# Moving the casts of expert 0's weights by three turns inside attention

## The chip, the cores and the metric

The kernel runs on one core of a Trainium2 chip. The metric is the time of one execution on the device in microseconds; the median of 3 runs of the kernel before is 624.77 us (624.53 to 625.55). Engine names: PE is TensorE (PEld its weight loads), DVE VectorE, ACT ScalarE, POOL GpSimd, SP SyncE.

## The reference

Three layers follow one another on 2 sequences of 768 tokens:

```
scores = q @ k.T / sqrt(64) + bias;  a = softmax(scores, masked)     # 8 heads, the last 96 keys and 8 global ones
x = a @ v                                                            # (2, 768, 512)
e = argmax(x @ w_gate), or the expert of the token before            # 8 experts, one per token
x = p[e] * (relu(x @ w1[e]) @ w2[e])
u = x + real(fft(fft(x, axis=1), axis=2))
out = u + relu(layernorm(u) @ w_ch1) @ w_ch2
```

All in float32. The expert of a token depends on a scan over the sequence.

## The kernel before

Attention works on 24 units, numbered n from 0 to 23: a unit is one tile of 128 queries (i, six of them), one sequence (b) and one half of the heads (g, four heads). The loop at L292 is software-pipelined: in its pass n it issues `scores` (PE, L152) and `rowmin` (DVE, L161) of unit n, the exponentials `expo` (ACT, four at L170, with `den` on POOL at L171 right behind them), the transposes `transp` (PE, L180) of unit n-1 in two halves, each copied out of PSUM by ACT (`out`, L186, tile `p`), the products with v (PE, L194) of unit n-2, and the turning back of unit n-3 (`keep` on DVE, L199, tile `o`; `upright` on PE, L204; `norm` on DVE). Every engine runs its instructions in the order in which the program issues them, so the place of a call in this loop is its place in the queue of its engine.

Four times in a pass, `step(k)` is called, with k = 4 (n - 24) and the three numbers after it: these are the four turns of a unit, 0 to 3. Turn 0 lies between `scores` and `expo`, turn 1 after the first `out`, turn 2 after the second half of `transp`, turn 3 at the end of the pass. In a turn, `bg.step()` advances every background generator by one step, the oldest first. Two kinds of generators are of interest:

- `route.run(i)` (L486), one per tile of queries, added after the last unit of a tile has been normalised, which is in turn 2 of pass 4i+6. It finds the expert of each token. For tiles 0 to 3 part of it is on POOL: `gn` (L532, read by PE at L551), `pe` (L548, read by ACT at L556), `su` (L562, read by DVE at L569), `oh` (L571), `xrow` (L593) and two indirect DMAs to `list` (L607). It waits for given turns (`to`, `at`).
- `ring.take("e", g, cols=512, eng=POOL)` (L1005), for expert 0's pieces g = 0, 1, 2. A piece is 128 x 2048 floats of weights in a raw buffer, loaded by DMA earlier (SP, L990). It is split into a rounded high part, a cast on ACT (L1052), and a low part, a subtraction on POOL (L1054), in four parts of 512 columns: cast, subtraction, cast, subtraction, one per turn. After the last subtraction the raw buffer's next load is issued. The high and low parts are first read by PE after attention, at L897.

`TAKES` (L672) says at which k each of the three generators is added. With (-53, -37, -21) this is turn 3 of passes 10, 14 and 18, so the casts fall in turns 3, 1, 3, 1 and the subtractions in turns 0, 2, 0, 2.

After attention the routing of the last tile, the scattering of tokens to the experts' lists, the eight experts, the Fourier step and the last layer follow.

Of the kernel before, what the change touches and what calls it, by code (L numbers as in the profile page):

```python
# [80 lines left out]
def fast_attention(tc, st, io, route):  # L81
# [4 lines left out]
    with ExitStack() as ctx:  # L86
# [189 lines left out]
        def step(k):  # L276

            for at, g in TAKES:
                if k == at:
# [389 lines left out]
EARLY_READ = 7  # L669
EARLY_GATHER = 6  # L670
LATE = 4
TAKES = ((-53, 0), (-37, 1), (-21, 2))  # L672
SPLIT = 6
WARM = 6, 6, 3
TOKENS = 4
# [1282 lines left out]
```

## Time and profile before

| | |
|---|---|
| median of 3 runs | 624.77 us |
| the profiled execution's own time | 628.3 us |
| its span, first to last instruction | 626.5 us |
| PE busy in the span | 606.2 us (97%) |
| DVE busy | 382.9 us (61%) |
| ACT busy | 274.1 us (44%) |
| POOL busy | 100.7 us (16%) |

Busy shares are means over stages with different limits: POOL is busy for 13.20 us of the 20 between 40 and 60 us, and nearly idle after 200 us. Times in the rows are counted from the span's start. In a timeline row stand start, length, engine, line, operation, tiles written and read, their shapes, the number of instructions merged into the row, and in brackets how long the engine had been idle before it and what released it. Lengths of instructions that follow one another on an engine overlap a little.

### The profile page before, as it was taken

The page shows a single profiled execution, that of the slowest core. Times are in us where ns is not written, and L with a number is a line of the kernel's source. Part 1 is how long each engine was busy: PE and PEld are TensorE (multiplying, and loading weights), DVE is VectorE, ACT ScalarE, POOL GpSimd, SP SyncE. Part 2 cuts the span into 40 slices and gives each one's busy share as a digit, 9 for nine tenths or more (in the row PEclk, how much of TensorE's full clock was granted, in tenths as well). Part 3 has the DMA queues.
Part 4 walks back from the last instruction along what each step waited for, and adds up shares of the span by engine and source line. Part 5 has one row for each costly group of instructions (what it writes and reads, how often), then busy time and mean ns, then how long its engine had stood idle before and what let it go on. Part 6 is the DMA issues. An engine that isn't in the chain of part 4 may idle for free.

```text
span 626.5 us, 9659 instructions
## 1 busy us (share of the span) xinstructions
PE 606.2 (97%) x3515; PEld 493.5 (79%) x3516; DVE 382.9 (61%) x897; ACT 274.1 (44%) x547; POOL 100.7 (16%) x149
## 2 busy tenths in 40 slices
PE   8999988899999899999999999999999999999997
PEld 4777875598898788887767887888888888888885
DVE  6788775569876958671499979997430221372112
ACT  6889883166564766573344534431211221131010
POOL 2146652324224033300000000000000000000000
PEclk9999999999999899999999999999999999999999
DMA  8568761399979788980450343560100100100001
GB/s 285 194 197 210 205 118 61 56 336 336 385 273 329 248 293 309 322 281 9 184 186 2 135 154 116 201 202 0 68 1 1 68 0 1 67 1 1 0 1 67
DMA packets 25186, 92.44 MB, mean 148 GB/s; under 512 B 7644, under 2 KB 8796, under 8 KB 17184
## 3 DMA queue, kind: packets, MB, share of 16 engines
q1 hardware_dynamic: 19664, 79.50, 38.4%
q0 software_dynamic: 4736, 10.56, 4.6%
q10 hardware_dynamic: 720, 1.55, 0.7%
q8 instruction: 34, 0.56, 0.4%
q14 instruction: 32, 0.26, 0.2%
HBM read 81.00 MB, written 14.84 MB: 153 GB/s over the span
## 4 chain that ended last, share of the span: by engine, by line
PE 51%; DVE 1%; ACT 0%; issue 0%; DVEq 0%; ACTq 0%
PE h L1759 21%; PE acc L1774 7%; PE acc L1775 7%; PE acc L1776 7%; PE y L1211 1%; PE acc L1593 1%; PE acc L1579 1%; PE h L1261 1%; PE f L1725 1%; PE f L1622 1%; PE h L52 1%; PE f L1644 0%; DVE u L1785 0%; PE acc L1582 0%; PE f L1625 0%; PE acc L1644 0%
## 5 line engine op out<-in xcount | busy, mean ns | idle before, releaser
L1764 DVE SCALAR_TENSOR_TENSOR hl<-h,hh 128x512 fp32r<-128x512 f32 x48 | 33.0, 688 | 118.0 <-ACT hh L1763 118.0
L1763 ACT ACTIVATE hh<-h 128x512 fp32r<-128x512 f32 x48 | 28.7, 598 | 164.9 <-PE h L1759 164.9
L1054 DVE TENSOR_TENSOR wide<-raws,wide 128x1024 fp32r<-128x1024 f32 (+1 forms) x38 | 44.7, 1198 | 28.9 <-ACT wide L1052 23.1
L170 ACT ACTIVATE t<-t,nm 128x256 f32<-128x256 f32 (+1 forms) x96 | 45.8, 479 | 10.9 <-DVE nm L161 10.1
L1052 ACT CAST wide<-raws 128x1024 fp32r<-128x1024 f32 (+2 forms) x42 | 40.7, 992 | 8.6 <-DMA raws<-wm 4.3
L1759 PE MATMUL h<-un0h,wide 128*128 128x512 f32 (+1 forms) x136 | 42.4, 378 | 0.1
L1774 PE MATMUL acc<-wide,hh 128*128 128x512 f32 (+1 forms) x97 | 37.9, 391 | 0.0
L1775 PE MATMUL acc<-wide,hh 128*128 128x512 f32 (+1 forms) x97 | 37.9, 390 | 0.0
L1776 PE MATMUL acc<-wide,hl 128*128 128x512 f32 (+1 forms) x97 | 37.6, 388 | 0.0
L161 DVE CUSTOM_DVE_ANT_0 t<-sp,bias 128x256 f32<-128x256 f32 (+1 forms) x96 | 32.8, 397 | 7.7 <-PE sp L152 3.8
L1140 POOL DMA_INDIRECT xg<-xs,ent x23 | 27.5, 1197 | 44.1 <-DVE pc L1187 21.4
L1759 PEld LDWEIGHTS h<-un0h,wide 128*128 128x128 f32 x136 | 25.0, 188 | 5.0 <-ACT un0h L1534 0.3
L180 PE MATMUL tp<-consts,t 128*128 128x128 f32 x176 | 26.2, 284 | 2.8 <-ACT p L186 2.8
L180 PEld LDWEIGHTS tp<-consts,t 128*128 128x128 f32 x176 | 18.6, 141 | 10.6 <-ACT p L186 6.6
L1759 PE MATMUL h<-un0l,wide 128*128 128x512 f32 (+1 forms) x68 | 25.6, 377 | 0.0
L194 PE MATMUL sm<-p,vs 128*64 128x128 f32 x352 | 24.5, 280 | 0.0
L186 ACT COPY p<-tp 128x512 f32<-128x512 f32 (+1 forms) x48 | 24.2, 534 | 0.3 <-PE tp L180 0.3
L1231 PE MATMUL h<-xh,wide 128*128 128x256 f32 x160 | 22.6, 280 | 0.0
L1103 DVE SCALAR_TENSOR_TENSOR dec<-raws,dec 128x1024 int32<-128x1024 int32 x18 | 22.0, 1225 | 0.6
L1101 DVE SCALAR_TENSOR_TENSOR dec<-raws,dec 128x1024 int32<-128x1024 int32 x18 | 22.0, 1223 | 0.5
L194 PEld LDWEIGHTS sm<-p,vs 128*64 128x64 f32 x352 | 18.7, 136 | 3.7 <-issue 3.6
L1234 ACT ACTIVATE hh<-h 128x512 fp32r<-128x512 f32 x20 | 12.0, 599 | 21.6 <-PE h L1231 16.5
(474 smaller groups left out, 1606.6 us busy)
## 6 DMA issues: line engine op xcount, KB each, us to landing
raws<-we SPq DMA_DIRECT2D x32, 1024.0 KB
raws<-wm SPq DMA_DIRECT2D x17, 1024.0 KB
raws<-wmf SPq DMA_DIRECT2D x7, 1024.0 KB
wmf<-dec POOLq DMA_DIRECT2D x8, 512.0 KB
xs<-xrow SPq DMA_DIRECT2D x12, 260.0 KB
vs<-v SPq DMA_DIRECT2D x6, 512.0 KB
raws<-kq SPq DMA_DIRECT2D x3, 1024.0 KB
u<-x SPq DMA_DIRECT2D x6, 512.0 KB
```

What stands on the lines that cost most here:

```text
L161: V.tensor_tensor_reduce(out=u.t[:, x, :u.W], in0=u.sp[:, j, k, :u.W], in1=bias[:, 4 * u.g + x, u.b0:u.b0 + u.W], scale=-0.125, scalar=3.0 ...
L170: A.activation(u.t[:, x, :u.W], u.t[:, x, :u.W], AF.Exp, bias=u.nm[:, x:x + 1], scale=-1.0, accum_out=u.den[:, x])
L180: T.transpose(u.tp[k][:, j, c], u.t[:, 2 * k + j, c * P:(c + 1) * P], st.ident)
L194: T.matmul(turned[j * D:j * D + D, k], vs[:, ti % KS, u.h + 2 * k + j], u.p[:, 2 * k + j, c], start=c == 0, stop=c == len(tiles) - 1)
L1052: (first or nc.scalar.copy)(hi[:, cs], raw[:, cs])
L1054: (eng() if callable(eng) else eng or nc.vector).tensor_tensor(lo[:, cs], raw[:, cs], hi[:, cs].bitcast(F32), op=ALU.subtract)
L1759: nc.tensor.matmul(ps[:, c], a[:, k], x[:, k, c], start=n == 0, stop=n == 11)
L1763: nc.scalar.activation(hh, ps, AF.Relu)
L1764: nc.vector.scalar_tensor_tensor(hl, ps, 0.0, hh.bitcast(F32), op0=ALU.max, op1=ALU.subtract)
L1774: T.matmul(acc[c][:, d], hh[:, cs], h2[:, d], start=first, stop=False)
L1775: T.matmul(acc[c][:, d], hh[:, cs], l2[:, d], start=False, stop=False)
L1776: T.matmul(acc[c][:, d], hl[:, cs], h2[:, d], start=False, stop=last and d.stop == DM)
```

## The change

One line: each of the three generators is added three calls of `step` sooner, in turn 0 of the same pass. The casts then fall in turns 0, 2, 0, 2 (the first and third), the subtractions in turns 1, 3, 1, 3.

```
-TAKES = ((-53, 0), (-37, 1), (-21, 2))
+TAKES = ((-56, 0), (-40, 1), (-24, 2))
```

Since the generator of a piece is now added in turn 0 of pass 10, before `route.run(1)` in turn 2 of the same pass, it also stands before that one in the list that `bg.step()` goes through.

On POOL, around the first piece, the kernel before has this order; the first `den` is that of unit 10, `list` and its two DMAs belong to the routing of tile 0, `gn`, `pe` and `su` to that of tile 1, and `sl0l` is the low part of the piece:

```order
L171 TENSOR_SCALAR den<-den 128x4
L607 DMA list<-dest,pos 12416x2 x2
L532 TENSOR_SCALAR gn<-lg 128x16
L124 COPY raws<-gk 128x4x8
L1054 TENSOR_TENSOR sl0l<-raws,sl0h 128x512
L171 TENSOR_SCALAR den<-den 128x4
L548 TENSOR_TENSOR pe<-lg,m_709 128x16
L1054 TENSOR_TENSOR sl0l<-raws,sl0h 128x512 x2
L171 TENSOR_SCALAR den<-den 128x4
L562 TENSOR_SCALAR su<-su 128x2
```

And the changed kernel, from the same `den` to the same `su`:

```order
L171 TENSOR_SCALAR den<-den 128x4
L1054 TENSOR_TENSOR sl0l<-raws,sl0h 128x512
L607 DMA list<-dest,pos 12416x2 x2
L1054 TENSOR_TENSOR sl0l<-raws,sl0h 128x512
L532 TENSOR_SCALAR gn<-lg 128x16
L124 COPY raws<-gk 128x4x8
L171 TENSOR_SCALAR den<-den 128x4
L1054 TENSOR_TENSOR sl0l<-raws,sl0h 128x512
L548 TENSOR_TENSOR pe<-lg,m_713 128x16
L1054 TENSOR_TENSOR sl0l<-raws,sl0h 128x512
L171 TENSOR_SCALAR den<-den 128x4
L562 TENSOR_SCALAR su<-su 128x2
```

Two subtractions have moved ahead of `gn`, a third ahead of `pe`, and the fourth ahead of `su`'s `den`; before, one stood ahead of `pe`, three ahead of `su`'s `den` and the fourth behind `su`.

On ACT, before, from the exponentials of unit 10 to those of unit 12; `sl0h` is the high part of the piece, `rows` and the small `pe` belong to the routing of tile 1:

```order
L170 ACTIVATE t,den<-t,nm 128x256 x4
L186 COPY p<-tp 128x512
L1052 CAST sl0h<-raws 128x512
L186 COPY p<-tp 128x512
L170 ACTIVATE t,den<-t,nm 128x256 x4
L186 COPY p<-tp 128x512
L1052 CAST sl0h<-raws 128x512 x2
L186 COPY p<-tp 128x512
L555 COPY rows<-sm 16x256
L556 ACTIVATE pe<-pe 128x16
L170 ACTIVATE t,den<-t,nm 128x256 x4
```

And after, from the cast that now stands ahead of the exponentials of unit 10:

```order
L1052 CAST sl0h<-raws 128x512
L170 ACTIVATE t,den<-t,nm 128x256 x4
L186 COPY p<-tp 128x512
L1052 CAST sl0h<-raws 128x512
L186 COPY p<-tp 128x512
L1052 CAST sl0h<-raws 128x512
L170 ACTIVATE t,den<-t,nm 128x256 x4
L186 COPY p<-tp 128x512
L1052 CAST sl0h<-raws 128x512
L186 COPY p<-tp 128x512
L555 COPY rows<-sm 16x256
L556 ACTIVATE pe<-pe 128x16
```

The two casts that stood together between two copies of `p` are apart, two casts stand ahead of exponentials, and the fourth cast, which came after the exponentials of unit 12, comes before them. The order on PE, SP and DVE is the same in both kernels. The second and third piece move in the same way, four units later each.

## Rows read from the trace of the kernel before

**Rows 1.** Windows view, 40 to 60 us; columns: stretch, length, engines' busy times, PEclk, DMA share, GB/s.
```profile
core 0: us, PE busy (x) PEld busy (x) DVE busy (x) ACT busy (x) POOL busy (x), PEclk, DMA share, GB/s
40.00:60.00 20.00, 19.66 (x202) 15.30 (x196) 16.74 (x87) 18.25 (x60) 13.20 (x22) 1.00 0.72 196
```
**Rows 2.** Timeline of PE, first piece.
```profile
45.41 0.22 PE L551 MATMUL sm<-identb,gn 128*16 128x128 bf16 x1
...
46.61 0.66 PE L180 MATMUL tp<-consts,t 128*128 128x128 f32 x4 [0.34 <-ACT p L186]
...
48.73 1.13 PE L152 MATMUL sp<-raws 64*128 64x256 f32 x8
...
52.70 1.13 PE L152 MATMUL sp<-raws 64*128 64x256 f32 x8
```
**Rows 3.** Timeline of ACT, first piece: exponentials of units 10 to 13 and two casts.
```profile
38.63 0.51 ACT L170 ACTIVATE t<-t,nm 128x256 f32<-128x256 f32 x1 [0.80 <-DVE nm L161]
...
42.49 0.51 ACT L170 ACTIVATE t<-t,nm 128x256 f32<-128x256 f32 x1 [0.32 <-DVE nm L161]
...
44.94 1.14 ACT L1052 CAST sl0h<-raws 128x512 fp32r<-128x512 f32 x2
...
46.83 0.49 ACT L170 ACTIVATE t<-t,nm 128x256 f32<-128x256 f32 x1
...
50.71 0.51 ACT L170 ACTIVATE t<-t,nm 128x256 f32<-128x256 f32 x1 [0.35 <-DVE nm L161]
```
**Rows 4.** Timeline of POOL, first piece.
```profile
40.86 0.23 POOL L171 TENSOR_SCALAR den<-den 128x4 f32<-128x4 f32 x1 [2.97 <-ACT t L170]
41.84 1.19 POOL L607 DMA_INDIRECT list<-dest,pos  x1 [0.76 <-DVE gf L539]
43.34 0.98 POOL L607 DMA_INDIRECT list<-dest,pos  x1 [0.30 <-issue]
44.32 0.31 POOL L532 TENSOR_SCALAR gn<-lg 128x16 bf16<-128x16 f32 x1
...
44.71 1.30 POOL L1054 TENSOR_TENSOR sl0l<-raws,sl0h 128x512 fp32r<-128x512 f32 x1
46.10 0.23 POOL L171 TENSOR_SCALAR den<-den 128x4 f32<-128x4 f32 x1
46.41 0.22 POOL L548 TENSOR_TENSOR pe<-lg,m 128x16 f32<-128x16 f32 x1
46.58 2.62 POOL L1054 TENSOR_TENSOR sl0l<-raws,sl0h 128x512 fp32r<-128x512 f32 x2
49.29 0.22 POOL L171 TENSOR_SCALAR den<-den 128x4 f32<-128x4 f32 x1
49.59 0.23 POOL L562 TENSOR_SCALAR su<-su 128x2 f32<-128x2 f32 x1
```
**Rows 5.** Timeline of DVE, first piece: the instruction that waits for su.
```profile
49.85 0.17 DVE L569 RECIPROCAL su<-su 128x2 f32<-128x2 f32 x1 [1.01 <-POOL su L562]
```
**Rows 6.** Timelines of POOL and PE, second and third piece: den, gn and L551.
```profile
56.70 0.23 POOL L171 TENSOR_SCALAR den<-den 128x4 f32<-128x4 f32 x1 [2.75 <-ACT t L170]
...
59.79 0.29 POOL L532 TENSOR_SCALAR gn<-lg 128x16 bf16<-128x16 f32 x1
...
61.27 0.22 PE L551 MATMUL sm<-identb,gn 128*16 128x128 bf16 x1
...
72.85 0.23 POOL L171 TENSOR_SCALAR den<-den 128x4 f32<-128x4 f32 x1 [3.42 <-ACT t L170]
...
75.94 0.28 POOL L532 TENSOR_SCALAR gn<-lg 128x16 bf16<-128x16 f32 x1
...
77.39 0.22 PE L551 MATMUL sm<-identb,gn 128*16 128x128 bf16 x1
```
**Rows 7.** Timeline of DVE, third piece: the copy of o behind L569.
```profile
83.64 0.42 DVE L199 COPY o<-sm 128x256 f32<-128x256 f32 x1 [1.66 <-PE tp L180]
```
**Rows 8.** Windows view of two microseconds after attention: clock and PE.
```profile
108.00:109.00 1.00, 1.00 (x3) 0.81 (x4) 0.61 (x2) 0.00 (x0) 0.71 (x1) 0.50 0.45 168
124.00:125.00 1.00, 0.00 (x0) 0.00 (x0) 1.00 (x1) 0.00 (x0) 0.00 (x0) 1.00 0.72 262
```
**Rows 9.** Windows view, 37.0 to 37.5 us: DMA traffic.
```profile
37.00:37.50 0.50, 0.50 (x6) 0.46 (x8) 0.50 (x2) 0.50 (x2) 0.41 (x2) 1.00 0.23 98
```

## The prediction

> **What bounds the kernel now.** I first read the windows view by stage, since the edit touches only the stretch from 37 to 84 us of the span. There TensorE is busy 19.66 of 20 us, ScalarE 18.25, VectorE 16.74 and GpSimd 13.20 [rows 1]; GpSimd's share of the whole span is small, but in this stretch it is two thirds. Then I read the timeline of one unit around expert 0's first piece, engine by engine. A unit's PE work, from one `scores` to the next, is about 4 us (48.73 to 52.70) [rows 2]. Where PE stops in it, it stops for ScalarE: the second half of the transposes at 46.61 stood 0.34 us for the copy of `p`, and that copy stood behind two casts in a row, 1.14 us from 44.94 [rows 2, 3]. GpSimd's work in these units is not slack either: gn (L532), pe (L548) and su (L562) of the routing lie in its queue, and PE (L551), ScalarE (L556) and VectorE (L569) wait for them. GpSimd runs its queue in order, so what stands ahead of these three counts.
>
> **The change part by part.** Nothing is added or removed. Per piece, four casts (a pair takes 1.14 us) and four subtractions on GpSimd move three turns up; this happens three times. The pieces' next loads stand where they stood in SP's queue and are released earlier.
>
> ScalarE's side is a gain. No two casts stand together between the halves of a `p` copy any more, so the copy at the end of the pair comes one cast sooner, and PE's 0.34 us go. The moved casts now stand ahead of the exponentials. There ScalarE was idle 0.80 us in unit 10 and 0.32 us in unit 11, waiting for nm [rows 3]; a cast takes half the pair, 0.57 us, of which the first is hidden whole and the second costs at most 0.25 us of ScalarE.
>
> GpSimd's side is the cost. Before, unit 10's queue is den, two L607, gn, and only then a subtraction. Now one subtraction stands between den and the first L607, a second between the last L607 and gn, and a third between the next den and pe. I rebuild the queue of the first piece [rows 4]. Den at 40.86; the step from den to the next instruction is 0.31 us (46.10 to 46.41): first subtraction at 41.17. It takes 1.30: end 42.47. L607 after 0.30 of issue (the idle of its second row): 42.77 instead of 41.84, since the 0.76 us that GpSimd idled there hide a part. From the first L607 to gn it was 2.48 us (41.84 to 44.32), so the second subtraction begins at 45.25; with 1.30 and 0.09 to the next instruction (46.01 to 46.10), gn begins at 46.64 and ends at 46.95, 2.32 us later than before.
>
> - PE: L551 stood at 45.41 [rows 2]; it cannot start before 46.95, 1.54 us later, and the transposes, `upright`, `values` and next `scores` queue behind it on PE. The 0.34 us of waiting for `p` are absorbed in this, so `scores` at 48.73 comes 1.20 us later. This is the lower end.
> - ScalarE: gn to the next group was 0.39 us (44.32 to 44.71), so den follows at 47.03, the third subtraction at 47.34, pe at 48.73 to 48.95 [rows 4]. The exp of pe (L556) stands in ScalarE's queue right ahead of the exponentials of unit 12; these begin 0.1 us after it, about 49.1 instead of 46.83 [rows 3]: 2.27 us later. This is the upper end.
> - VectorE: den before came at 49.29, 2.46 us after those exponentials began, 0.39 of it because a subtraction ended only at 49.20. Now the last subtraction (48.9 to 50.2) is over in time: den 51.2, su 51.5, and L569, which came 0.26 us after su began, 51.8 instead of 49.85 [rows 4, 5]. Behind L569 stand the copy of `o`, for which PE's `upright` waits, and the next `rowmin`, for which the exponentials of unit 13 (50.71) wait [rows 3]. PE has some 0.5 us between that copy and its `upright`, so unit 14's `scores` (52.70) [rows 2] comes about 1.5 us later. Unit 13 has no cast left and no second subtraction, and PE works through it without a wait, so little is won back there.
>
> I take 1.5 us per piece, between 1.2 and 2.3. The second and third piece stand the same way: gn came 3.09 us after den both times, 3.46 in the first; by the same steps gn moves from 59.79 to about 62.4 and from 75.94 to about 78.6, past L551 at 61.27 and 77.39 [rows 6]. For the third piece I take 1.0 only: behind its L569 VectorE stands 1.66 us more, until 83.64, for a reason that the trace does not give (the named PE instructions were begun and the copy usually follows at once) [rows 7]. If that wait ends at a fixed moment, the delay disappears in it; if it has a fixed length, it stays. Sum: 1.5 + 1.5 + 1.0 = 4.0 us. After attention everything hangs on its last unit (routing, list, gathers), so I pass the 4.0 us on whole.
>
> The profiled execution took 628.3 us (span 626.5 and 1.8 around it), 3.5 above the median of the runs, 624.77. 632.3 over 628.3 is 1.0064; on the median that is 628.8 us. Bounds of the mechanism: 2.4 us (two pieces at the lower end, the third lost in that wait) to 6.9 (three at the upper end): 627.2 to 631.7.
>
> **The rivals.**
>
> 1. Faster. The pair of casts is the only thing that PE waits for, and GpSimd's lateness reaches nobody. Then each piece wins PE's 0.34 us of waiting and up to the 0.57 us of one cast, about 0.43 us: 1.3 us in all, 623.5 us. For it: the wait for `p` is PE's only visible one in unit 12, and GpSimd idles long ahead of den. Against it: den stays ahead of the first subtraction, so that idle time cannot be used, and gn would have to be done at 45.41, that is, lose 0.78 us at most; I count 2.32. It decides from there.
> 2. No change: the ScalarE gain and a GpSimd delay of under one subtraction cancel, 624 to 625.5 us. This needs gn's delay to be about 1.2 us, half of what I find; subtractions beside other engines' work would have to be shorter than their rows.
> 3. A slower clock. TensorE has a hole of 1.5 us per piece. At 108 us its granted clock is 0.50, the 1.2 GHz level, after several microseconds in which it was often idle; but from 124 to 125 us it was idle for the whole microsecond and stayed at 1.00 [rows 8]. I expect no fall. If it fell in each piece for the about 3.5 us of the stretch at 108, PE would lose half of that, 1.75 us, three times: 634 us.
> 4. The first cast now wants its data at 37.8 us. The load of that piece runs together with others; traffic has fallen to 98 GB/s at 37.0 to 37.5 [rows 9], so I take it as landed. Should it land 1 us late, the first cast would hold back exponentials that start at 38.63 by 0.7 us, once: 629.5 us, inside the forecast's range.
>
> On rival 3, the Trainium skill ("TensorE: Matmul & The Clock Gate", Part 1: The HAM clock gate) says that a gate halves the matmul clock after the array has been idle and gives it back after sustained work. By that rule a change that opens holes in TensorE's work pays twice, as worked out in rival 3 from rows; this trace agrees for 108 us and shows no fall for the hole at 124.
>
> **How the numbers follow.** A difference under 0.2%, 1.25 us, cannot be told from none. The forecast has 0.81 (628.8 us, almost all of it above 626.0), rival 1 has 0.09, rival 2 has 0.06, rival 3 has 0.04; rival 4 is inside the forecast. So faster 0.09, same 0.07 (rival 2 and the forecast's lowest edge), slower 0.84. The range runs from 625.3 to 631.5. Its low end lies below the mechanism's 627.2, since a wait as that of [rows 7] may swallow the loss of a second piece too; left out are rival 1, rival 3 and the outermost of the bounds.
>
> **What would show it.** In the timeline of the changed kernel, in each of the three pieces: gn starts about 5.8 us after the den that precedes it (3.1 to 3.5 before); L551 waits for GpSimd, PE empty for about 1.5 us ahead of it; L556 waits for pe on GpSimd and the four exponentials behind it begin 2.3 us late; L569 comes 1.9 us late; no wait of the transposes for a `p` copy behind two casts. The windows view from 37 to 90 us should take about 4 us longer for the same instructions, and from the last unit on nothing should change but the start. I am wrong if L551 starts without a wait for GpSimd, if the stretch is not longer, or if the loss is given back between 97 and 125 us, where the end of attention is handed to the routing.

## The result, and the profile after

The changed kernel takes 627.52 us (median of 13 runs, 626.58 to 630.71) where the kernel before took 624.77 beside it: 1.0058 times as long over all runs, 95% interval 1.0039 to 1.0076 (the quotient of the medians is 1.0044). It is slower, by 3.6 us at the ratio's middle, near the forecast (1.0064). One of the 13 executions of the kernel before took 988.36 us and is left out of the ratio.

The two profiled executions don't show this in their spans, 627.0 and 626.5 us: the one of before was a long one (3.5 us above its median, as the prediction noted). So I compare the stretch that the change touches, by the starts of `scores` (PE, L152) of units 11, 14, 15, 18, 19, 22 and 23, and beside it a second execution of the kernel before, the first experiment below. All in us:

| kernel | 11 to 14 | 15 to 18 | 19 to 22 | 11 to 23 |
|---|---|---|---|---|
| before, the profile shown | 12.08 | 12.35 | 13.45 | 49.15 |
| before, second execution | 12.08 | 12.35 | 12.49 | 48.20 |
| after | 13.53 | 13.59 | 13.39 | 51.78 |

51.78 less 48.20 is 3.58 us, the size of the ratio. First the windows view of the changed kernel, which answers to [rows 1]:

```profile
core 0: us, PE busy (x) PEld busy (x) DVE busy (x) ACT busy (x) POOL busy (x), PEclk, DMA share, GB/s
40.00:60.00 20.00, 18.26 (x178) 13.81 (x174) 16.40 (x75) 17.11 (x53) 12.16 (x21) 1.00 0.70 195
```

PE lost 1.40 us of its 19.66, at an unchanged clock of 1.00. Where, the timeline of PE around the first piece shows [rows 2] (times in this trace read about 0.17 us lower: the first `den` is at 40.69 instead of 40.86):

```profile
42.89 0.77 PE L204 MATMUL mi<-iw,o 128*128 128x148 f32 x4 [0.18 <-issue]
...
44.62 1.14 PE L152 MATMUL sp<-raws 64*128 64x256 f32 x8
46.52 0.22 PE L551 MATMUL sm<-identb,gn 128*16 128x128 bf16 x1 [0.77 <-POOL gn L532]
...
49.28 1.13 PE L152 MATMUL sp<-raws 64*128 64x256 f32 x8
51.20 1.14 PE L180 MATMUL tp<-consts,t 128*128 128x128 f32 x8 [0.79 <-ACT p L186]
52.17 0.67 PE L204 MATMUL mi<-iw,o 128*128 128x148 f32 x4
...
53.97 1.14 PE L152 MATMUL sp<-raws 64*128 64x256 f32 x8
```

Beside a short stop of 0.18 there are two holes where there was one of 0.34: 0.77 for gn at L551, and one unit later 0.79 for the copy of `p`. The queue of GpSimd, against [rows 4]:

```profile
40.69 0.23 POOL L171 TENSOR_SCALAR den<-den 128x4 f32<-128x4 f32 x1 [2.96 <-ACT t L170]
41.00 1.27 POOL L1054 TENSOR_TENSOR sl0l<-raws,sl0h 128x512 fp32r<-128x512 f32 x1
42.45 1.19 POOL L607 DMA_INDIRECT list<-dest,pos  x1 [0.17 <-DVE fr L537]
43.94 0.98 POOL L607 DMA_INDIRECT list<-dest,pos  x1 [0.30 <-issue]
44.92 1.31 POOL L1054 TENSOR_TENSOR sl0l<-raws,sl0h 128x512 fp32r<-128x512 f32 x1
46.17 0.30 POOL L532 TENSOR_SCALAR gn<-lg 128x16 bf16<-128x16 f32 x1
...
46.70 0.23 POOL L171 TENSOR_SCALAR den<-den 128x4 f32<-128x4 f32 x1
47.00 1.28 POOL L1054 TENSOR_TENSOR sl0l<-raws,sl0h 128x512 fp32r<-128x512 f32 x1
48.24 0.22 POOL L548 TENSOR_TENSOR pe<-lg,m 128x16 f32<-128x16 f32 x1
48.42 1.27 POOL L1054 TENSOR_TENSOR sl0l<-raws,sl0h 128x512 fp32r<-128x512 f32 x1
50.84 0.22 POOL L171 TENSOR_SCALAR den<-den 128x4 f32<-128x4 f32 x1 [1.15 <-ACT t L170]
51.14 0.23 POOL L562 TENSOR_SCALAR su<-su 128x2 f32<-128x2 f32 x1
```

Gn comes 5.48 us after den (3.46 before), with the two subtractions between them; pe waits for the third. GpSimd is hardly idle from den to the fourth subtraction's end. The same den, gn and L551 of the second and third piece, from the timelines of GpSimd and PE [rows 6]:

```profile
57.97 0.23 POOL L171 TENSOR_SCALAR den<-den 128x4 f32<-128x4 f32 x1 [2.58 <-ACT t L170]
...
63.30 0.28 POOL L532 TENSOR_SCALAR gn<-lg 128x16 bf16<-128x16 f32 x1
...
63.63 0.22 PE L551 MATMUL sm<-identb,gn 128*16 128x128 bf16 x1 [0.57 <-POOL gn L532]
...
75.36 0.23 POOL L171 TENSOR_SCALAR den<-den 128x4 f32<-128x4 f32 x1 [2.80 <-ACT t L170]
...
80.67 0.30 POOL L532 TENSOR_SCALAR gn<-lg 128x16 bf16<-128x16 f32 x1
...
81.03 0.22 PE L551 MATMUL sm<-identb,gn 128*16 128x128 bf16 x1 [0.60 <-DVE nm L161]
```

Gn comes 5.33 and 5.31 us after den, against 3.09 twice. PE stops ahead of L551 here too, 0.57 and 0.60 us (for the third the profile names nm, but gn ended at 80.97, right ahead of 81.03), and one unit later 0.75 and 0.78 for `p`. And ScalarE [rows 3]:

```profile
43.21 0.51 ACT L170 ACTIVATE t<-t,nm 128x256 f32<-128x256 f32 x1 [0.69 <-DVE nm L161]
...
45.66 0.61 ACT L1052 CAST sl0h<-raws 128x512 fp32r<-128x512 f32 x1
...
48.49 0.22 ACT L556 ACTIVATE pe<-pe 128x16 f32<-128x16 f32 x1 [1.30 <-POOL pe L548]
48.62 0.49 ACT L170 ACTIVATE t<-t,nm 128x256 f32<-128x256 f32 x1
...
52.26 0.51 ACT L170 ACTIVATE t<-t,nm 128x256 f32<-128x256 f32 x1 [0.63 <-DVE nm L161]
```

No pair of casts is left, and the cast ahead of the exponentials at 43.21 did not hold them up: ScalarE waited 0.69 us for nm behind it. What holds ScalarE is L556, 1.30 us idle for pe, with the four exponentials of unit 12 behind it; their lateness is the second hole of PE. On VectorE, L569 [rows 5], the place of [rows 7], and one row that I had not thought of:

```profile
41.23 1.06 DVE L537 CAST fr<-ix 128x2 f32<-128x2 uint32 x1
...
51.40 0.17 DVE L569 RECIPROCAL su<-su 128x2 f32<-128x2 f32 x1 [0.73 <-POOL su L562]
...
85.90 0.17 DVE L569 RECIPROCAL su<-su 128x2 f32<-128x2 f32 x1 [0.73 <-POOL su L562]
85.98 0.40 DVE L199 COPY o<-sm 128x256 f32<-128x256 f32 x1
```

In the third piece the copy of `o` follows L569 at once: the wait of 1.66 us of [rows 7] is not there. And the cast to `fr`, of 128 x 2 elements, took 1.06 us. In the kernel before, the timeline of VectorE has it so:

```profile
41.41 0.17 DVE L537 CAST fr<-ix 128x2 f32<-128x2 uint32 x1
```

The slow one ended at 42.29, with the subtraction that now runs beside it (41.00 to 42.27). Behind it on VectorE stands the copy of `o` for which PE's `upright` (L204) waits: the short stop of 0.18, which is gone in the run below that computes `fr` later.

### The profile page after: what moved, and what is told of

Same layout as the page of the kernel before. It is cut to its first block, busy times and chain, and to the rows that moved or that the text cites. A ratio compares the mean times of both kernels' runs of the same rounds, so it can differ in the third digit from the quotient of the medians.

```text
span 627.0 us, 9656 instructions
## 1 busy us (share of the span) xinstructions
PE 604.7 (96%) x3515; PEld 492.6 (79%) x3516; DVE 386.9 (62%) x897; ACT 274.4 (44%) x547; POOL 101.2 (16%) x149
## 4 chain that ended last, share of the span: by engine, by line
PE 51%; DVE 1%; ACT 0%; issue 0%; DVEq 0%; ACTq 0%
PE h L1759 21%; PE acc L1775 7%; PE acc L1774 7%; PE acc L1776 7%; PE y L1211 1%; PE acc L1593 1%; PE acc L1579 1%; PE h L1261 1%; PE f L1725 1%; PE f L1622 1%; PE h L52 1%; PE f L1644 0%; DVE u L1785 0%; PE acc L1582 0%; PE f L1625 0%; PE acc L1644 0%
## 5 line engine op out<-in xcount | busy, mean ns | idle before, releaser
L1763 ACT ACTIVATE hh<-h 128x512 fp32r<-128x512 f32 x48 | 28.8, 599 | 164.4 <-PE h L1759 164.4
L1774 PEld LDWEIGHTS acc<-wide,hh 128*128 128x128 f32 x97 | 18.2, 188 | 4.0
```

Source lines behind the costliest of these rows:

```text
L1763: nc.scalar.activation(hh, ps, AF.Relu)
L1774: T.matmul(acc[c][:, d], hh[:, cs], h2[:, d], start=first, stop=False)
```

## The experiments

The theory: the loss is the place of the subtractions in GpSimd's queue, ahead of gn and pe. Its rival: the casts ahead of the exponentials hold up ScalarE, and GpSimd's lateness reaches nobody. Stretches are those of the table above; a time without a ratio is a single one, and single times scatter (12 executions of the kernel before lie between 622.40 and 626.84 us), so there the stretches decide.

**The kernel before once more** (no edit).

> The kernel before once more, for a second profile. In the first, the three stretches from scores of unit 11 to 14, 15 to 18 and 19 to 22 took 12.08, 12.35 and 13.45 us, the third with a wait of 1.66 us behind L569 that the trace did not explain; the granted clock fell from 108 to 111 us. Theory (the wait belongs to this order of instructions): it is there again, third stretch 13.4 us, and the third piece really costs nothing in the changed kernel. Rival (it belongs to that one execution): third stretch about 12.0 us, and the changed kernel's 13.39 us is a loss of 1.4 us as in the other two.

623.26 us; stretches 12.08, 12.35, 12.49. The hole behind L569 is not at L199 this time but behind it, ahead of `rowmin`, and 0.72 us long. It belongs to an execution, not to the kernel, and the third piece's cost is to be counted from 12.49 rather than 13.45.

**The casts alone three turns sooner**, every subtraction where the kernel before has it.

```diff
+def casts(g):            # hi: high part, raw: raw buffer
+    for c in range(0, PW, 512):
+        A.copy(hi[:, c:c + 512], raw[:, c:c + 512])
+        yield
+        yield
...
+if k == at - 3: bg.add(casts(g))
 if k == at: bg.add(take(..., first=lambda hi, raw: None))
```

> Casts in the changed kernel's turns, subtractions in those of the kernel before: the order on POOL is that of before, the order on ACT that of the changed kernel. Theory (the loss comes from gn and pe standing behind subtractions on POOL): no loss; PE's wait for p behind two casts is gone, so 0.3 to 0.5 us less per piece than before, stretches 11.6 to 11.8 us, 623.5 us in all. Rival (the casts ahead of the exponentials hold ACT up): stretches as in the changed kernel, 13.4 to 13.6 us, 628 us.

621.93 us, 0.9975 of before (0.9956 to 0.9994); stretches 11.67, 12.61, 11.63. ScalarE's order is that of the changed kernel, and the kernel is not slower but a little faster: the rival falls. Only the second stretch is not shorter but 0.26 longer. There ScalarE (first fence; L279 is the cast in this kernel), and for it PE, waits:

```profile
54.43 0.62 ACT L279 CAST sl1h<-raws 128x512 fp32r<-128x512 f32 x1 [0.65 <-DMA raws<-we]
```

```profile
57.55 0.66 PE L180 MATMUL tp<-consts,t 128*128 128x128 f32 x4 [0.33 <-ACT p L186]
58.55 0.66 PE L180 MATMUL tp<-consts,t 128*128 128x128 f32 x4 [0.35 <-ACT p L186]
```

The first cast of the second piece waited for its load (the prediction's rival 4, at another piece), and the exponentials behind it came late. In the changed kernel no cast waits for a load.

**Routing ahead of the piece in each turn**: the three generators of the changed kernel stand in a list of their own that is stepped after the others.

```diff
+bg, late = Background(), Background()
-bg.add(ring.take(...))
+late.add(ring.take(...))
 bg.step()
+late.step()
```

> The changed kernel, but in each turn the routing goes before the piece: the second subtraction then stands behind gn and the third behind pe; only the first still stands ahead of the two L607. Theory: gn comes 0.9 us late instead of 1.85 to 2.5 (L551 then waits 0.1 to 0.3 us for it) and pe about 1 us late; 0.4 to 0.6 us lost per piece, stretches 12.2 to 12.6 us, 626 us. Rival (ACT): as the changed kernel, 13.4 to 13.6 us, 628 us.

623.71 us, 1.0002 (0.9987 to 1.0018); stretches 12.46, 12.82, 12.34. With gn and pe ahead of their turn's subtraction, most of the loss is gone though casts and subtractions fall in the changed kernel's turns.

**GpSimd's lateness without the moved casts**: the kernel before, and per piece two more subtractions of 512 columns, whose result nothing reads. In GpSimd's queue both stand between den and the first L607, ahead of gn and so of pe.

```diff
+if k in (at - 2, at):
+    G.tensor_tensor(spent, full[:, :512], full[:, 512:1024], op=ALU.subtract)
```

> The kernel before with two more subtractions of 128x512 on POOL per piece, whose results nobody reads, issued in turns 1 and 3 of passes 10, 14 and 18, so that gn and pe come as late as in the changed kernel, while the casts stay as they were. Theory (POOL): stretches of 13.5 to 14.0 us, L551 waits for gn and L556 for pe as in the changed kernel, 629 to 630 us. Rival (ACT, or the moved casts): stretches as before, 12.1 to 12.4 us, 625 us.

627.61 us, 1.007 (1.0042 to 1.0097); stretches 14.17, 14.19, 14.00. The timeline of PE shows the same two holes, and the one behind the pair of casts on top (L556 is the multiplication on gn here):

```profile
46.52 0.22 PE L556 MATMUL sm<-identb,gn 128*16 128x128 bf16 x1 [0.91 <-POOL gn L537]
51.20 0.66 PE L180 MATMUL tp<-consts,t 128*128 128x128 f32 x4 [0.76 <-ACT p L186]
52.20 0.66 PE L180 MATMUL tp<-consts,t 128*128 128x128 f32 x4 [0.34 <-ACT p L186]
```

Gn comes 5.60 us after den and pe 7.68, close to the changed kernel's 5.48 and 7.55. So lateness of gn and pe on GpSimd costs 2.1, 1.8 and 1.5 us per piece with no cast moved (against the second execution of before). The cast to `fr` is held up here too (1.04, 0.99 and 0.78 us), so this run does not part the two; the one with VectorE's flags later, below, does.

**One piece alone**: only the first, or only the third, is taken sooner.

```diff
-TAKES = ((-53, 0), (-37, 1), (-21, 2))
+TAKES = ((-56, 0), (-37, 1), (-21, 2))     # and, apart, ((-53, 0), (-37, 1), (-24, 2))
```

> Only the first piece is taken three turns sooner, the second and third stand as in the kernel before. Theory (each piece pays by its own order on GpSimd): the stretch from unit 11's scores to unit 14's is 13.4 to 13.6 us as in the changed kernel (12.08 before), with L551 waiting for gn once, and the other two stretches are those of the kernel before, 12.3 to 12.4 and 12.4 to 13.5. Rival (the pieces hang together, by the loads that the first one releases): the second and third stretch differ from the kernel before's by more than 0.3 us, or the first stretch is below 13.2.

> Only the third piece is taken three turns sooner. Theory: the first two stretches are 12.1 and 12.35 us as before, and the third, from unit 19's scores to unit 22's, is 13.3 to 13.5 with a wait of L551 ahead of it, 0.9 longer than in the second execution of the kernel before (12.49). The hole of 1.66 us at L199 does not come back, since it belonged to one execution. Rival (the third piece costs nothing, its delay falls into that hole): the stretch is 12.5 to 12.7 and the hole of 1.0 to 1.7 us stands behind L569.

Stretches 13.51, 12.33, 12.33 for the first alone (623.12 us), and 12.09, 12.34, 13.38 for the third alone (626.55 us; behind unit 23 this execution took 2.5 us longer than the second one of before). Each piece pays for itself: 1.43 for the first, 1.05 for the third (13.38 less 12.33).

**The casts at two distances**: as the casts alone, but the second piece's one turn sooner instead of three.

```diff
+if k == at - (1 if g == 1 else 3): bg.add(casts(g))
```

> The casts of the first and third piece are taken three turns sooner, those of the second one turn sooner; all subtractions on GpSimd stand where the kernel before has them. Theory (the casts' new places are a gain, the second piece's first cast only came too soon for its load): the three stretches are 11.7, 11.9 and 11.6 us, no cast waits for a DMA, and the time is 0.3 to 0.6% under the kernel before, about 621 us. Rival (what was won with the casts alone is ScalarE's place ahead of the exponentials, equal for all turns): the second stretch stays at 12.6 and the time is that of the casts alone, 0.25% under the kernel before.

621.19 us, 0.997 (0.9951 to 0.9988); stretches 11.87, 11.91, 11.63. The second piece's cast no longer waits for its load, but in this execution the first piece's did (timeline of ScalarE), and the first stretch is 0.20 longer than with the casts alone:

```profile
38.23 0.62 ACT L279 CAST sl0h<-raws 128x512 fp32r<-128x512 f32 x1 [0.50 <-DMA raws<-we]
```

The kernel is a little faster than the kernel before; from the casts alone (0.9975) the times don't tell it apart, but the second stretch does, 11.91 against 12.61.

**The first piece's subtractions eight turns later**, casts as in the casts alone.

```diff
+if k == at - 3: bg.add(casts(g))
+if k == at + (8 if g == 0 else 0): bg.add(take(...))
```

> All casts three turns sooner, and the first piece's four subtractions on GpSimd eight turns later than in the kernel before. It tests why the load of the second piece was not there. Theory (transfers run slowly beside the subtractions): with no subtraction from 44 to 51 us of the span, the traffic there is 300 to 400 GB/s where it was 40 to 100, the second piece's load lands at about 50 instead of 53.5 us, and its first cast waits for nothing; the traffic falls later, at 52 to 58 us, where the subtractions now stand. Rival (traffic is low there for another reason, such as small packets of that load or the indirect DMAs): 40 to 100 GB/s from 47 to 51 as before, and the first cast of the second piece waits about 0.65 us.

The windows view (last two columns: share of the DMA engines, GB/s) and ScalarE's first cast of the second piece:

```profile
48.00:49.00 1.00, 1.00 (x12) 0.77 (x10) 0.20 (x1) 1.00 (x4) 0.35 (x2) 1.00 1.21 66
...
50.00:51.00 1.00, 1.00 (x10) 0.85 (x10) 1.00 (x7) 1.00 (x5) 1.00 (x1) 1.00 0.62 106
51.00:52.00 1.00, 1.00 (x20) 0.83 (x18) 0.90 (x4) 1.00 (x6) 0.20 (x1) 1.00 0.97 410
```

```profile
53.66 0.62 ACT L279 CAST sl1h<-raws 128x512 fp32r<-128x512 f32 x1 [0.64 <-DMA raws<-we]
```

622.23 us; stretches 11.50, 12.92, 11.63. My theory here (transfers run slowly beside the subtractions) fell. With hardly a GpSimd instruction from 45 to 48.6 us the traffic was as low as with three subtractions, and the cast still waited 0.64 us. The load was issued at 44.74 and waited for until 53.66, 8.9 us (45.15 to 54.43 with the casts alone, 9.3), whatever GpSimd did. That agrees with the Trainium skill ("SBUF — State Buffer", Who interferes with whom), by which a DMA never contends with a compute engine. The issuing instruction on SP took 2.55 us of it (44.74 to 47.29), where that of the load at 30.11 took 0.92; from 47 to 51 us only 57 to 106 GB/s moved at DMA shares of 0.37 to 1.21. Why stays open.

**Gn, and gn with pe, on VectorE**: two kernels, the changed one with one line or two lines edited.

```diff
-X.tensor_scalar(gn, ...)        # X: GpSimd
+V.tensor_scalar(gn, ...)        # V: VectorE
...
-X.tensor_tensor(pe, ...)        # in the second kernel alone
+V.tensor_tensor(pe, ...)
```

> The changed kernel with gn computed on VectorE instead of GpSimd. Theory (two waits in a row, both behind the subtractions: L551 for gn, then the exponentials behind L556 for pe): the wait of L551, 0.77 us, goes, but pe comes only about 0.3 us sooner, the length of gn, so the wait of the transposes for the copy of p grows from 0.79 to about 1.2 us; the stretch from unit 11's scores to unit 14's falls from 13.53 to 13.2 only. Rival (gn's lateness alone is the loss, and the second wait only follows from it): the second wait stays at 0.8 or falls, and the stretch is 12.8 or less.

> The changed kernel with gn and pe computed on VectorE, so that of the routing's values that PE and ScalarE wait for none stands behind a subtraction; casts and subtractions stand as in the changed kernel. Theory (the loss is the order on GpSimd): both waits go, the three stretches are 11.7 to 12.1, 11.9 to 12.6 (the second piece's first cast may wait for its load, since the exponentials are early again) and 11.6 to 12.0 us, and the time is below the kernel before's by 0 to 2 us. Rival (the casts' places ahead of the exponentials hold up ScalarE, and so PE): a wait of 0.5 us or more of the transposes for the copy of p stays in each piece, and the stretches are 12.5 or more.

Gn alone: stretches 13.34, 13.41, 13.16 (626.96 us). The wait for gn is gone and the one for `p` behind pe grew from 0.79 to 0.90 with a wait of 0.27 in the unit ahead of it: only 0.2 us are won, so the two waits stand in a row. Gn and pe: 12.43, 12.79, 13.49 (625.12 us). L556 starts without a wait, the first two stretches give back most of the loss, but the first is not down to 11.7 to 12.1, and the third gives nothing back. There pe on VectorE was held up beside GpSimd's work instead; from this kernel the timelines of VectorE, GpSimd and PE:

```profile
76.84 1.99 DVE L548 TENSOR_TENSOR pe<-lg,m 128x16 f32<-128x16 f32 x1
```

```profile
76.51 0.98 POOL L607 DMA_INDIRECT list<-dest,pos  x1 [0.30 <-issue]
77.49 1.30 POOL L1054 TENSOR_TENSOR wide<-raws,wide 128x512 fp32r<-128x512 f32 x1
```

```profile
79.94 0.22 PE L551 MATMUL sm<-identb,gn 128*16 128x128 bf16 x1 [1.48 <-DVE o L199]
```

A subtraction of 128 x 16 elements, 0.17 us long in the first piece, began beside an indirect DMA, 0.65 us ahead of the GpSimd subtraction, and ended at 78.83, with that subtraction (78.79). PE waited 1.48 us for what stood behind it.

**VectorE's flags later**: is VectorE's hold-up, seen at L537, a cost of its own in the changed kernel? `fr` and `gf` are computed with pe instead of at once; in a second kernel so with gn and pe on VectorE too.

```diff
-if X is G:
-    for _ in flags:
-        pass
```

> The changed kernel with fr and gf (VectorE, L537 and L539) computed one turn group later, with pe, instead of right behind the search for the expert. In the changed kernel the cast to fr took 1.06 us instead of 0.17, since it ran beside the subtraction that now stands behind den, and it ended with it; VectorE's next rowmin and unit 11's exponentials came 0.9 us late for that. Theory (GpSimd's queue alone sets gn, and VectorE's hold-up only fills part of the same wait): the cast takes 0.17 to 0.2 where no subtraction runs, the wait of L551 for gn grows from 0.77 to about 1.2 us, and the first stretch stays at 13.4 to 13.7 us. Rival (VectorE's hold-up is a cost of its own that adds to gn's): the first stretch falls by 0.4 to 0.5, to 13.0 to 13.1, and the wait for gn stays at 0.8.

> The changed kernel with gn and pe on VectorE and fr and gf one turn group later. With gn and pe alone on VectorE the first stretch was 12.43 us, 0.76 above the 11.67 of the kernel with the casts alone moved. Theory (that rest is VectorE held beside subtractions: the cast to fr took 1.15 there): the first stretch falls to 11.7 to 12.0. In the third piece pe itself was held on VectorE for 1.99 us beside the indirect DMAs and a subtraction; it stands in the same place, so the third stretch stays above 13.0 unless the later fr and gf move it. Rival (the rest is the casts' place or GpSimd's su): the first stretch stays at 12.3 to 12.5.

The changed kernel with the flags later: 13.51, 13.61, 13.37 (626.33 us), the stretches of the changed kernel within 0.02. Of it the timelines of PE and VectorE (line numbers from L540 on are three lower):

```profile
46.45 0.22 PE L548 MATMUL sm<-identb,gn 128*16 128x128 bf16 x1 [1.21 <-POOL gn L532]
51.11 1.14 PE L180 MATMUL tp<-consts,t 128*128 128x128 f32 x8 [0.77 <-ACT p L186]
```

```profile
43.05 0.16 DVE L537 CAST fr<-ix 128x2 f32<-128x2 uint32 x1
```

The cast is short again, and PE waits for gn 1.21 us instead of 0.77: what VectorE no longer takes, gn takes. In the changed kernel VectorE's hold-up fills a part of the same hole. With gn and pe on VectorE as well the stretches are 12.15, 12.79 and 12.05 (623.27 us): the first and third fall by 0.28 and 1.44 against the kernel with gn and pe alone moved, so there the hold-up was a cost. The first stays 0.15 above what I expected; in it the scan, which now runs beside a subtraction from its start (47.07), took 1.45 us where the kernel before had 1.03:

```profile
47.16 1.45 DVE L563 TENSOR_TENSOR_SCAN ex<-rows,ex 16x128 f32<-16x128 f32 x1
```

## Why the prediction was right

Point by point, in its order; times of after are moved by the 0.17 us of its zero.

- ScalarE's gain is real: 0.41 us in the first piece (12.08 to 11.67 with the casts alone) and 0.25% of the time (0.06 to 0.44%), near the 0.43 per piece of rival 1. Rival 1 failed where it was said to decide: at gn.
- Gn was 2.02 us late in the first piece, forecast 2.32 (5.48 after den instead of 5.8). The order was as rebuilt; the term too large was the pauses between instructions: 0.17 ahead of the first L607 instead of 0.30, and none between the second subtraction and gn.
- L551 came 1.28 us late (forecast 1.54), the exponentials behind L556 1.96 (2.27), L569 1.72 (1.9). All three are short by 0.2 to 0.3 us, which is gn's error handed on.
- PE's hole ahead of L551 was to be about 1.5 us and is 0.77. This step was mis-sized. The runs show what was missing: VectorE is held up beside the first subtraction, `scores` of unit 12 come 0.45 us late for it, and gn is then waited for that much less; without the hold-up the hole is 1.21. `scores` of unit 13 came 0.72 us late, forecast 1.20 as the lower end: L551 was 1.28 us late, and from the transposes behind it to L204 it took 0.93 us instead of 1.49, 0.56 less where I had taken off 0.34. I had not said that PE would stop a second time, 0.79, for the `p` copy of the late exponentials, though their lateness was the upper end. 0.77 and 0.79 and 0.18 at L204 less the 0.34 that went are 1.40 us, and the stretch grew by 1.45.
- Unit 14's `scores` came 1.44 us late, forecast about 1.5, but not by the path I gave, L569 and the copy of `o`: `upright` at 52.17 followed the transposes without a wait, and what PE waited for was `p`. That 1.5 came out is in part luck: one hole was half as long as I said, and the other I had not counted.
- Per piece I took 1.5, 1.5 and 1.0. Measured: 1.45, 1.24 and 0.90 (1.05 with the third piece alone), 3.59 in all for 4.0. The third was right by luck: the wait at [rows 7] was not there to swallow anything; it did not come back at that place in any other run. The second and third piece lost less than the first though gn came later in them, 2.24 and 2.22 us against 2.02, since gn had more room there: before, it was done 1.19 and 1.17 us ahead of L551, in the first 0.78 [rows 2, 4, 6].
- The loss was passed on from the last unit: 3.58 us in the stretch, and 3.6 by the ratio (2.4 to 4.7). From unit 23's `scores` to the first transposes for the experts (PE, L883) is 8.92 us in the changed kernel and 8.75 in the second execution of before, and to the first `cnt` (VectorE, L648, at 112.75) 20.53. The six other executions whose granted clock stayed at 1.00 up to there took 20.33 to 20.60, the seven in which it fell to 0.50 on the way, both of the kernel before among them, 21.39 to 22.00. So the two kernels' traces can't be compared there without the clock.
- Rival 2 needed a gn delay of 1.2 us, and it was 2.0. Rival 3: the clock stayed at 1.00 through the stretch, with holes of 0.8 us. Rival 4 did not happen in the changed kernel, but four runs with the casts three turns sooner had such a wait at the second piece (0.42 to 0.65 us), and the one with the casts at two distances had it at the first (0.50).

What is shown: that the subtractions' place ahead of gn and pe costs the time (without the moved casts it costs more than the change; with these two ahead, or off GpSimd, most of it goes), and that the casts' new places cost nothing but a wait for a load that is late. What is not settled: why that load is slow.

## What to carry to other kernels

Before moving work of two engines together, rebuild the queue of each: here the half on ScalarE was worth a gain of 0.25%, and the half on GpSimd a loss of about three times that (0.7% without the moved casts), because small results that two other engines wait for stand in the same queue. An engine that is idle a third of a stretch can still be late at the one moment that counts. And where two waits stand in a row, removing one of them is worth little: see who waits next.

## What was not expected of the hardware

VectorE's short instructions are held up beside GpSimd's subtractions (both inputs in SBUF, 1.27 to 1.31 us). The cast of 128 x 2 elements to `fr` mostly took 0.17 us with none running and 0.78 to 1.15 where it fell wholly beside one, and ended with it; the scan to `ex` 0.47 to 1.45, while the copies of `o` out of PSUM took 0.39 to 0.43 us throughout. The Trainium skill ("SBUF — State Buffer", Who interferes with whom) states it: VectorE in a two-port mode, or with two inputs in SBUF beside a GpSimd instruction that reads SBUF, contends with GpSimd for a port pair, and the later of the two blocks until the other is done. The casts to `fr` agree with it, and by that rule the prediction should have read not only GpSimd's queue but what VectorE does beside each of its new places; here gn's wait hid that cost.

GpSimd's indirect DMAs seem to hold VectorE up at times too. Where the tensor subtraction `pe` took 1.99 us instead of 0.17, it had begun beside one, ahead of the GpSimd subtraction with which it ended. In the changed kernel with the flags later, the cast to `fr` of the second piece ended with an indirect DMA (60.67 and 60.69); its timelines of VectorE and GpSimd:

```profile
60.31 0.36 DVE L537 CAST fr<-ix 128x2 f32<-128x2 uint32 x1
```

```profile
59.63 1.06 POOL L604 DMA_INDIRECT list<-dest,pos  x1 [0.16 <-issue]
```

Other casts beside an indirect DMA took 0.17 us, so when this happens is not shown.
